# Two mixed attentions on one core: scores as a half-array and a quarter-array product, two heads at a time, and part of the local attention moved into the projections

## The chip, the core and the metric

The kernel runs on one core of a Trainium2 chip. The core has TensorE (matmuls, `PE` in the profile, its weight loads `PEld`), VectorE (`DVE`), ScalarE (`ACT`), GpSimd (`POOL`), and SyncE (`SP`), whose queue issues nearly all DMAs here. The metric is the device time of one execution in microseconds, the median of several runs.

## The reference

`x` has 2048 rows of 448. Two multi-head attentions of 16 heads of 28 are computed from it, with weights of their own, and mixed by a gate:

```python
g = sigmoid((x * gate_w).sum(-1, keepdims=True))
a = A(x, A_wqkv, A_wo)      # local: each position sees 8 positions, itself and every second one before it
b = B(x, B_wqkv, B_wo)      # full: softmax(q k^T / sqrt(28)) v over all 2048 positions
out = g * a + (1 - g) * b
```

## The kernel before

**Precision.** A matmul operand is split into a high part in a rounded 32-bit type (`F32R`) and a low part, the rest. A product is the sum of three: high x high, high x low, low x high. The product of attention weights and values alone is a plain float32 matmul, which the profile counts as two instructions.

**Projections.** 92 tiles in the order of a list `tiles`: 28 of q and k of B, transposed (`qk_tile`), 16 of v of B (`v_tile`), 48 of q, k, v of A (`a_tile`). Each is 11 matmuls (`project`, `L241`) into one of four PSUM banks `R`, copied out by ScalarE. q and k of B go to DRAM in two parts (`qk_hi`, `qk_lo`), those of A to `a_scr`. From tile 11 on each tile is followed by `s1_quad`: four matmuls of 28 rows in the four row groups of the array (`s1_mm`, `L121`), one per head, into a four-bank tile, and one VectorE maximum over the four banks (`s1_max`, `L125`). These are approximate scores, from the high parts alone, for the row maxima that the softmax subtracts. The gate's sum is a VectorE multiply-and-sum per tile of 128 rows (`gate_tile`, `L288`), from `x` loaded once more by rows.

**Main stage.** A loop over 16 units `u` (a group of four heads, a block of 512 queries) and 16 key tiles `kt` of 128 keys: 256 steps. In a step, `scores` computes S = K Q for four heads, each 128 keys x 512 queries in one PSUM bank. A head's q and k lie in one group of 32 partitions: 28 rows of values and, in the first product, two more, where k holds ones and q the negated row maximum in its two parts. So a head is three matmuls of a quarter of the array (30, 28, 28 rows), and matmuls of different row groups run at once. Three maxima matmuls of a later unit run between them, each with its VectorE maximum, until they are done: 64 a unit are 1024, 80 x 4 = 320 come in the projections, and the other 704 take 235 steps. The order is written out by hand, first digit the head, second the product, `s` a maximum:

```python
WITH = "10 20 s0 11 21 00 30 12 22 31 01 s1 32 02 s2".split()
ALONE = "00 10 20 30 01 11 21 31 02 12 22 32".split()
```

ScalarE takes the exponential of each bank into SBUF (`L885`). `do_av` then multiplies the previous step's four tiles with V (`L851`): four heads in four column groups, 128 rows each. Seven banks rotate through `order`: a step's scores and maxima take them in the order in which the step before had used them.

**Local attention.** It runs beside the main stage, in 8 chunks of two heads: GpSimd multiplies q with each of 8 shifted k (`a_score`, `L491`) and for some adds the two halves of the products (`L496`); VectorE sums the rest in two or four reduces (`a_reduce`, `L501`); then a softmax over the 8 (`a_softmax`); then GpSimd multiplies with v and sums up (`a_av`, `L541`, `L546`). Each such operation is an item in a list per engine, with a sort key, a cost, and the items that it needs with a least distance in steps. `issue` takes, at each step, the items whose needs are met, as long as the engine's planned lateness (`late`), which falls by a planned step (2.3) each step, stays under a limit: 4.2 us for GpSimd, 0.7 for VectorE.

**End.** From two steps after the last maximum, `op_some` puts seven items of the output products into each step (`op_mm`, `L693`), and the rest follows behind the loop. Loads of the finished attention rows (`op_load_b`) are tied to fixed steps, `READY` holds items back to a step.

Of the kernel before, what the change touches and what calls it, by code (L numbers as in the profile page):

```python
# [11 lines left out]
ALU = mybir.AluOpType  # L12
# [13 lines left out]
def gated_mix_kernel(ctx: ExitStack, tc: tile.TileContext, xT, xn, gw, wA, wB, woAB, out):  # L26
# [19 lines left out]
    pp = ctx.enter_context(tc.tile_pool(name="pp", bufs=16))  # L46
# [7 lines left out]
    T = []  # L54

# [16 lines left out]
    KH = [cp.tile([128, S], F32R, name=f"KH{i}") for i in range(2)]  # L72
    KL = [cp.tile([128, S], F32R, name="KL0")]
# [6 lines left out]

    def ptile(name):
        return pp.tile([128, 512], F32, tag="P", name=name)
# [5 lines left out]
    def load_k(g, t, src):  # L88
        for h in range(4):
            r = D + 112 * g + DH * h  # L90
            dma_r(t[32 * h:32 * h + DH, :], src[r:r + DH, :])

    def load_part(u, name, src):
        g, b = divmod(u, NB)
        t = sp.tile([128, 512], F32R, name=name)
        for h in range(4):
            r = 112 * g + DH * h
            dma_r(t[32 * h:32 * h + DH, :], src[r:r + DH, 512 * b:512 * b + 512])
        return t

    Qs = {}

    def load_q(u):
        Qs[u] = load_part(u, "QH", qk_hi), load_part(u, "QL", qk_lo)
        for i in range(2):
            dma_r(Qs[u][0][DH + i::32, :], nm[u][16 * i:16 * i + 16, :].rearrange("(h q) c -> h (q c)", h=4))
# [4 lines left out]
    s1c = [0]  # L111
    s1e = 64 * NU
    finished = []

    def s1_mm(n, bank):
        u, i = divmod(n, 64)
        qs, kc, h = i // 16, i // 4 % 4, i % 4
        if i == 0 and u + 1 < NU:
            qhis[u + 1] = load_part(u + 1, "qhi", qk_hi)
        r = slice(32 * h, 32 * h + DH)  # L120
        nc.tensor.matmul(bank, qhis[u][r, 128 * qs:128 * qs + 128],  # L121
                         KH[u // NB % 3][r, 512 * kc:512 * kc + 512], start=True, stop=True)

    def s1_max(n, k, bank):
        nc.vector.tensor_reduce(MX[:, n % NMX:n % NMX + k], bank, axis=X, op=ALU.max)  # L125
        if n // 64 != (n + k) // 64:
            finished.append(n // 64)
        s1c[0] = n + k

    def s1_quad():  # L130
        n = s1c[0]
        for i in range(4):
            s1_mm(n + i, T[0][:, i, :])
        s1_max(n, 4, T[0])
# [20 lines left out]
    def max_store(u, r):  # L155
        for a in range(4):
            nc.sync.dma_start(nm[u].bitcast(F32)[:, 32 * a:32 * a + 32], r[32 * a:32 * a + 32, :])

# [7 lines left out]
    with tc.tile_pool(name="xp", bufs=1) as xp, tc.tile_pool(name="wp", bufs=2) as wp:  # L166
# [35 lines left out]
        def load_w(wi, tails=(False, True)):  # L202
            src, cols = WSRC[wi]
            if wi not in wraw:
                wraw[wi] = raw3(), ptile("wt"), sum(c1 - c0 for c0, c1 in cols)
            r, t, _ = wraw[wi]
            for tail in tails:
                o = 0
# [7 lines left out]

        def split_w(wi, kts):
            if wi not in wsets:
                wsets[wi] = [wp.tile([128, 4, 448], F32R, tag=g, name=f"{g}{wi}") for g in ("wh", "wl")]
            wh, wl = wsets[wi]  # L220
            r, t, n = wraw[wi]
            for kt in kts:
                split(wh[:, kt, :n], wl[:, kt, :n], r[:, kt, :n] if kt < 3 else t[:, :n], nc.gpsimd)
# [38 lines left out]
        def v_tile(j, ws):  # L262
            bank = next_bank()
            project(bank[:, :D], j // 4, slice(128 * (j % 4), 128 * (j % 4) + 128), ws, slice(0, D), False)
            nc.scalar.activation(V[:, j, :, 0:DH], bank[:, :D].rearrange("p (h d) -> p h d", d=DH), AF.Copy)
# [3 lines left out]
        def a_tile(i, j, ws):  # L269
            bank = next_bank()  # L270
            project(bank[:, :D], j // 4, slice(128 * (j % 4), 128 * (j % 4) + 128), ws, slice(0, D), False)
# [3 lines left out]
            nc.scalar.activation(stage[0][:, :, j % 2, :], bank[:, :D].rearrange("p (c e) -> p c e", e=56), AF.Copy)  # L275
            if j % 2 == 1:
                nc.sync.dma_start(a_own[i][:, :, j - 1:j + 1, :].rearrange("c p j e -> p c j e"), stage[0])

        gwt = cp.tile([128, D], F32, name="gwt")
        gx = {}  # L280

        def gate_load(j):
            gx[j] = ptile("xg")
            nc.sync.dma_start(gx[j][:, :D], xn[:, j, :])

        def gate_tile(j):
            jk = ptile("xj")
            nc.vector.scalar_tensor_tensor(jk[:, :D], gx.pop(j)[:, :D], 1.0, gwt, op0=ALU.mult, op1=ALU.mult,  # L288
                                           accum_out=zt[:, j:j + 1])
# [4 lines left out]
        WSRC = [None, (wB, [(128, 448), (832, 896)]), (wB, [(704, 832)]),  # L294
                (wB, [(896, 1344)]), (wA, [(0, 448)]), (wA, [(448, 896)]), (wA, [(896, 1344)])]

        wh0 = wp.tile([128, 4, 448], F32R, tag="wh", name="wh0")
        wl0 = wp.tile([128, 4, 448], F32R, tag="wl", name="wl0")
# [45 lines left out]
        for i, k, nb in ([(0, k, nb) for nb, k in ((0, 1), (0, 0), (0, 2), (1, 1), (1, 2), (1, 0), (2, 1), (3, 1),  # L344
                                                   (2, 0), (2, 2), (3, 0), (3, 2))]
                         + [(i, k, nb) for i in (1, 2) for nb in range(NB) for k in range(len(QK[i]))]):
            tiles.append((i, "qk", nb, QK[i][k], 128 * k))
        for j in range(NJ):
            tiles.append((3, "v", j))
        for i in range(3):  # L350
            for j in range(NJ):
                tiles.append((4 + i, "a", i, j))
# [6 lines left out]
        loads = {2: 17, 3: 22, **{wi: firsts[wi - 1] for wi in (4, 5, 6)}}  # L359
        splits = {1: firsts[1] - 4, 2: firsts[2] - 4, 3: firsts[3] - 4, **{wi: firsts[wi - 1] + 2 for wi in (4, 5, 6)}}  # L360
        for n, t in enumerate(tiles):
# [4 lines left out]
            for w in splits:  # L366
                if splits[w] <= n < splits[w] + 2:
                    split_w(w, (2 * (n - splits[w]), 2 * (n - splits[w]) + 1))
            if n == 1:
# [8 lines left out]
            else:  # L378
                a_tile(t[2], t[3], ws)
            if n in (2, 3):  # L380
                load_w(1, (n == 3,))
            if n == 4:
                init_kh(KH[0])
            if n == 7:
                load_k(0, KH[0], qk_hi)
                qhis[0] = load_part(0, "qhi", qk_hi)
            if n == 8:
                nc.sync.dma_start(gwt, gw)
# [3 lines left out]
            if n == 9:  # L392
                init_kh(KH[1])
                nc.gpsimd.memset(V[:, :, :, DH:], 1.0)
            if n == 22:
                load_k(1, KH[1], qk_hi)
            if n == 62:
                load_k(0, KL[0], qk_lo)
# [3 lines left out]
            if finished and n < len(tiles) - 2:  # L402
                u = finished.pop(0)
                parts.append((u, max_parts(u)))
            if S1_START <= n < len(tiles) - 1:
                s1_quad()
            if 26 <= n < 58 and n % 2 == 0:
                gate_load((n - 26) // 2)
            if 29 <= n < 61 and n % 2 == 1:
                gate_tile((n - 29) // 2)  # L410
            if n == 64:
# [5 lines left out]
            if n == 65:  # L417
# [13 lines left out]

    hooks = {}

    def at(pos, st, f):
        hooks.setdefault((st, pos), []).append(f)

    def run(pos, st):
        for f in hooks.pop((st, pos), ()):
            f()


# [6 lines left out]

# [571 lines left out]
```

## Time and profile before

| | |
|---|---|
| median of 3 runs | 962.66 us (961.21 to 963.15) |
| profiled execution | 962.09 us, its span 960.3 us |
| granted TensorE clock | 0.996 |
| busy: PE, PEld | 947.0 us (99%), 553.0 us (58%) |
| busy: DVE, ACT, POOL | 746.2 (78%), 647.7 (67%), 521.9 (54%) |
| first and last score matmul (`L882`) | 280.8 us, 926.2 us after the start |

Busy time is the union of an engine's instructions. Matmuls overlap, so TensorE's 99% does not say that it is at its peak: what one slot of the array takes is read from the starts in the timeline. The busy share is a mean over stages with different limits, so the prediction reads each stage alone.

### The profile page before, as it was taken

Reading aid. Unit: us, or ns where it says so; the run is one execution under the profiler, and the core shown is the slowest. Engines: PE = TensorE matmul, PEld = TensorE weight load, DVE = VectorE, ACT = ScalarE, POOL = GpSimd, SP = SyncE. Lnnn points to the kernel's source line nnn. Section 1 sums busy time; section 2 is a strip of 40 time slices with the busy share of each in tenths; the row PEclk is TensorE's granted clock in tenths of the full one; section 3 lists DMA queues with packets and bytes.
Section 4 is the critical chain, followed back from the end, with each engine's and each line's share of the span. In section 5 each row is a group of like instructions: output and inputs, shape, how many; then the busy total and the mean of one; then the engine's idle time right before and its main releaser. Section 6 shows DMA issues by size and latency. Waiting matters only on the chain.

```text
span 960.3 us, 19993 instructions
## 1 busy us (share of the span) xinstructions
PE 947.0 (99%) x7578; PEld 553.0 (58%) x7578; DVE 746.2 (78%) x1166; ACT 647.7 (67%) x1309; POOL 521.9 (54%) x384
## 2 busy tenths in 40 slices
PE   8999999999999999999999999999999999999988
PEld 6766777777764544445444444444444444465657
DVE  6477888887779999999999999999998888400012
ACT  4434212122139999999999999999999999856541
POOL 1346101010018689999999999999993853100000
PEclk9999999999999999999999999999999999999999
DMA  9868414354246241314515331520312123344332
GB/s 277 284 199 251 137 48 126 108 135 127 77 117 212 67 126 50 89 47 118 157 42 124 108 88 37 167 72 22 107 43 51 33 68 111 111 141 127 110 102 90
DMA packets 102392, 108.15 MB, mean 113 GB/s; under 512 B 60844, under 2 KB 72636, under 8 KB 101400
## 3 DMA queue, kind: packets, MB, share of 16 engines
q1 hardware_dynamic: 102152, 106.62, 38.4%
q8 instruction: 59, 0.97, 0.4%
q10 hardware_dynamic: 144, 0.26, 0.1%
q14 instruction: 37, 0.30, 0.1%
HBM read 65.89 MB, written 40.48 MB: 111 GB/s over the span
## 4 chain that ended last, share of the span: by engine, by line
PE 87%; DMA 5%; DVE 3%; POOL 2%; SPq 1%; ACT 1%; issue 1%; ACTq 0%; DVEq 0%
PE av L851 25%; PE r L241 19%; PE r L882 15%; PE T L882 11%; PE T L121 6%; PE r L693 4%; PE T L693 4%; PE r L121 3%; DVE MX L125 2%; DMA kt<-a_scr 1%; DMA oal<-oa_scr 1%; PE r L671 1%; SPq L85 1%; POOL prod L541 1%; POOL oat L546 1%
## 5 line engine op out<-in xcount | busy, mean ns | idle before, releaser
L125 DVE TENSOR_REDUCE MX<-T 128x1 f32<-128x512 f32 (+1 forms) x384 | 384.6, 1021 | 59.6 <-PE T L121 54.5
L885 ACT ACTIVATE P<-r 128x512 f32<-128x512 f32 x581 | 329.8, 609 | 53.6 <-PE r L882 32.5
L125 DVE TENSOR_REDUCE MX<-r 128x1 f32<-128x512 f32 x400 | 262.5, 686 | 22.4 <-PE r L121 16.5
L851 PE MATMUL av<-P,V 128*32 128x512 f32 x2048 | 273.6, 606 | 0.4 <-ACT osb L708 0.4
L885 ACT ACTIVATE P<-T 128x512 f32<-128x512 f32 x443 | 255.7, 610 | 19.8 <-PE r L882 11.1
L121 PE MATMUL T<-KH,qhi 28*128 28x512 f32 x624 | 169.9, 475 | 0.9 <-DVE MX L125 0.6
L882 PE MATMUL r<-QH,KH 30*128 30x512 f32 x581 | 166.5, 471 | 1.2 <-ACT ast L275 0.6
L121 PE MATMUL r<-KH,qhi 28*128 28x512 f32 x400 | 162.6, 455 | 0.0
L882 PEld LDWEIGHTS r<-QH,KH 30*128 30x128 f32 x581 | 75.4, 183 | 125.5 <-DVE MX L125 111.3
L882 PE MATMUL T<-QH,KH 30*128 30x512 f32 x443 | 146.2, 472 | 1.0 <-ACT P L885 0.5
L882 PE MATMUL r<-QL,KH 28*128 28x512 f32 x581 | 141.8, 394 | 0.0
L882 PE MATMUL r<-QH,KL 28*128 28x512 f32 x581 | 141.4, 392 | 0.0
L491 POOL TENSOR_TENSOR prod<-qt,kt 128x896 f32<-128x896 f32 x64 | 135.0, 2114 | 7.1 <-DMA kt<-a_scr 7.0
L882 PE MATMUL T<-QL,KH 28*128 28x512 f32 x443 | 120.6, 395 | 0.0
L882 PE MATMUL T<-QH,KL 28*128 28x512 f32 x443 | 119.9, 392 | 0.0
L546 POOL TENSOR_TENSOR oat<-oat,prod 128x896 f32<-128x896 f32 x56 | 118.1, 2110 | 2.4
L882 PEld LDWEIGHTS T<-QH,KH 30*128 30x128 f32 x443 | 59.8, 182 | 91.5 <-DVE MX L125 86.5
L275 ACT ACTIVATE ast<-r 128x448 f32<-128x448 f32 x48 | 26.1, 545 | 106.7 <-PE r L241 102.3
L541 POOL TENSOR_TENSOR prod<-vt,L 128x896 f32<-128x896 f32 x56 | 95.5, 1705 | 0.7
L121 PEld LDWEIGHTS T<-KH,qhi 28*128 28x128 f32 x624 | 70.9, 182 | 35.9 <-DVE MX L125 27.6
L851 PEld LDWEIGHTS av<-P,V 128*32 128x32 f32 x2048 | 40.3, 108 | 67.6 <-issue 62.1
L681 DVE TENSOR_TENSOR oalo<-r,oah 128x384 fp32r<-128x384 f32 x16 | 8.9, 558 | 90.3 <-ACT onhi L680 80.6
(127 smaller groups left out, 1438.8 us busy)
## 6 DMA issues: line engine op xcount, KB each, us to landing
a_scr<-ast SPq DMA_DIRECT2D x24, 448.0 KB
qk_hi<-qkh SPq DMA_DIRECT2D x24, 256.0 KB
qk_lo<-qkl SPq DMA_DIRECT2D x24, 256.0 KB
rbc<-rs SPq DMA_DIRECT2D x60, 64.0 KB
KH<-qk_hi SPq DMA_DIRECT2D x16, 224.0 KB
qhi<-qk_hi SPq DMA_DIRECT2D x64, 56.0 KB
xg<-in_xn SPq DMA_DIRECT2D x16, 224.0 KB
KL<-qk_lo SPq DMA_DIRECT2D x16, 224.0 KB
```

Of the source, the lines that this page charges most:

```text
L85: nc.sync.dma_start(dst.bitcast(F32), src.bitcast(F32))
L121: nc.tensor.matmul(bank, qhis[u][r, 128 * qs:128 * qs + 128], KH[u // NB % 3][r, 512 * kc:512 * kc + 512], start=True, stop=True)
L125: nc.vector.tensor_reduce(MX[:, n % NMX:n % NMX + k], bank, axis=X, op=ALU.max)
L241: nc.tensor.matmul(bank, wa if wfirst else xa, xa if wfirst else wa, start=(i == 0), stop=(i == len(ORDER) - 1))
L275: nc.scalar.activation(stage[0][:, :, j % 2, :], bank[:, :D].rearrange("p (c e) -> p c e", e=56), AF.Copy)
L491: nc.gpsimd.tensor_tensor(out=p, in0=qt[c], in1=kvt["k", c % 2][:, HALO - DIL * w:HALO - DIL * w + NJ, :], op=ALU.mult)
L541: nc.gpsimd.tensor_tensor(out=dst.rearrange("p j (h d) -> p j h d", d=DH), in0=kvt["v", c % 2][:, HALO - DIL * w:HALO - DIL * w + NJ, :].r ...
L546: nc.gpsimd.tensor_tensor(out=oat[c], in0=oat[c], in1=oat[c, w], op=ALU.add)
L693: nc.tensor.matmul(bank[:, :D], src, wo[c][:, k, :], start=(first and k == ks[0] and i == 0), stop=(last and k == ks[-1] and i == 2))
L851: nc.tensor.matmul(av[32 * h:32 * h + 32, :], V[:, kt, 4 * g + h, :], tiles_[h], start=(kt == 0), stop=(kt == NJ - 1), skip_group_check=True)
L882: nc.tensor.matmul(held[a], (KH[g % 3], KH[g % 3], KL[g % 2])[t][r, ks], (qh, ql, qh)[t][r, :], start=(t == 0), stop=(t == 2))
L885: nc.scalar.activation(p, held[a], AF.Exp, scale=SCALE)
```

## The change

Three things are changed together.

1. **Scores.** The three products of a head become two. `wide`: a head's high and low k lie in two groups of 32 partitions next to each other, in one half of the array, with the high q beside both; one matmul of 60 rows (62 for two of the heads) sums high x high, low x high and the two rows of the maximum. `narrow`: high k x low q, 28 rows, in a quarter. Heads 0 and 1 have their tiles in one pair (`KT[..][0]`), heads 2 and 3 in another. A step does two heads first, then the other two, the pairs taking turns; the maxima matmuls use the row groups that `narrow` leaves free. K tiles now have two places, with one more (`KS`) for the maxima of group 2, and q has two places of three tiles (`QT`).
2. **Local scores of chunks 0 and 1 in the projections.** The projections' order changes: q and k of A for channels 0 to 3 (16 tiles) come after the first 12 tiles, V comes last. The local items with negative keys are issued from tile 28 on; their tiles lie in the place of V until V is written. GpSimd now adds halves once for even shifts (two reduces left) and twice for odd ones and for chunks 0 and 1 (one reduce left).
3. **Gate.** `gate_w` is two more columns of a projection's weights (450 columns); ScalarE copies the sum out.

With these go: a planned step of 2.2 for 2.3, an exponential buffer split into 11 and 5 tiles, K loads at other steps, and the output stage's loads and `READY[1, 3]` two to four steps later.

```diff
-    WITH = "10 20 s0 11 21 00 30 12 22 31 01 s1 32 02 s2".split()
-    ALONE = "00 10 20 30 01 11 21 31 02 12 22 32".split()
...
+        first = (0, 1) if st % 2 == 0 else (2, 3)
+        then = (2, 3) if st % 2 == 0 else (0, 1)
...
+        def wide(h):
+            held[h] = free.pop(0)
+            r = slice(0, 60) if h < 2 else slice(0, 62)
+            r = slice(r.start + 64 * (h % 2), r.stop + 64 * (h % 2))
+            nc.tensor.matmul(held[h], KT[g % 2][h // 2][r, ks], qa[h // 2][r, :], start=True, stop=False)
+
+        def narrow(h):
+            r = slice(HB[h], HB[h] + DH)
+            nc.tensor.matmul(held[h], KT[g % 2][h // 2][r, ks], ql[r, :], start=False, stop=True)
+            p = ptile("P")
+            nc.scalar.activation(p, held[h], AF.Exp, scale=SCALE)
+            cur[h] = p
...
+        for h in first:
+            wide(h)
+        for h in first:
+            narrow(h)
+        yield
+        if more_s1:
+            maxima(then[0], "s0")
+            maxima(then[1], "s1")
+        for h in then:
+            wide(h)
+        for h in then:
+            narrow(h)
+        if more_s1:
+            maxima(first[st // 2 % 2], "s2")
+            order[:] = [held[x] for x in (first[0], "s0", first[1], "s1", then[0], "s2", then[1])]
...
+    KT = [[cp.tile([128, S], F32R, name=f"K{i}{p}") for p in range(2)] for i in range(2)]
+    HB, LB = (0, 64, 32, 96), (32, 96, 0, 64)
...
+    def load_q(u):
+        t = QT[u % 2]
+        for p in range(2):
+            for base in (HB, LB):
+                load_part(u, t[p], qk_hi, base, (2 * p, 2 * p + 1))
+            for i in range(2):
+                dma_r(t[p][HB[2 * p] + DH + i::64, :],
+                      nm[u][16 * i + 8 * p:16 * i + 8 * p + 8, :].rearrange("(h q) c -> h (q c)", h=2))
+        load_part(u, t[2], qk_lo, HB)
...
+    at("pre", 12, lambda: load_k(2, qk_hi, HB, KS[0]))
+    for st, g, src, base in ((30, 1, qk_lo, LB), (72, 2, qk_hi, HB), (84, 2, qk_lo, LB),
+                             (129, 3, qk_hi, HB), (136, 3, qk_lo, LB)):
...
+        n = DH
+        for _ in range(3 - NR(c, w)):
+            n //= 2
+            nc.gpsimd.tensor_tensor(out=p[:, :, 0:n], in0=p[:, :, 0:n], in1=p[:, :, n:2 * n], op=ALU.add)
...
+    def NR(c, w):
+        return 1 if c < EC or w % 2 else 2
...
+        add_a(1)
+        tiles.extend((i, "qk", nb, rows, 128 * k) for i in (2, 3) for nb in range(NB) for k, rows in enumerate(QK[i]))
+        add_a(4)
+        add_a(5)
+        tiles.extend((6, "v", j) for j in range(NJ))
...
+            if n > D:
+                nc.scalar.activation(zt[:, j:j + 1], bank[:, D:D + 1], AF.Copy)
...
+            if n >= firsts[2]:
+                st = n - len(tiles)
+                if t[1] == "qk":
+                    late["pool"] += 1.3
+                issue("sp", st, 0)
+                if not any(0 <= n - splits[w] + 2 < 4 for w in splits):
+                    issue("pool", st, 5.2)
+                issue("dve", st, DLIM)
...
-    READY[1, 3] = OP0 + 22
+    READY[1, 3] = OP0 + 26
...
-            step = 2.3 if left else 2.1
+            step = 2.2 if left else 2.1
```

562 lines of the change are left out of this document (288 added, 274 removed).

## The prediction

> **What bounds the kernel now.** I read the page first, then the busy time by stage, then single steps in the timeline, then the groups by shape.
>
> ```profile
> PE 87%; DMA 5%; DVE 3%; POOL 2%; SPq 1%; ACT 1%; issue 1%; ACTq 0%; DVEq 0%
> ```
>
> This is the chain that ended last: 87% of it is TensorE. The later projections, and the main stage up to the end of the row maxima (behind it lie 109 us of steps with output products, and 28 us of end that the change doesn't touch):
>
> ```profile
> 139.00:281.00 142.00, 140.64 (x730) 105.28 (x731) 117.72 (x77) 31.54 (x66) 10.44 (x12) 1.00 0.42 114
> 281.00:823.00 542.00, 540.83 (x5351) 261.45 (x5349) 506.50 (x951) 497.65 (x994) 464.39 (x324) 1.00 0.32 90
> ```
>
> Columns are PE, PEld, DVE, ACT, POOL, granted clock, DMA share, GB/s. The second row is 56% of the span, with all four engines over 85% busy. The `av` products tell its steps (eight instructions each):
>
> ```profile
> 281.00:823.00 542.00, 247.76 (x1856) 36.56 (x1856) 1.00 0.32 90
> ```
>
> 1856/8 = 232 steps; 542/232 is 2.34, and without the 2 to 4 us of start-up about 2.32 us a step. One step on TensorE:
>
> ```profile
> 604.39 1.06 PE L851 MATMUL av<-P,V 128*32 128x512 f32 x8
> 605.38 0.50 PE L882 MATMUL r<-QH,KH 30*128 30x512 f32 x2
> ...
> 605.71 0.50 PE L882 MATMUL T<-QH,KH 30*128 30x512 f32 x1
> 605.72 0.40 PE L882 MATMUL r<-QL,KH 28*128 28x512 f32 x2
> ...
> 605.96 0.39 PE L882 MATMUL r<-QH,KL 28*128 28x512 f32 x1
> ...
> 606.20 0.38 PE L121 MATMUL T<-KH,qhi 28*128 28x512 f32 x1
> ...
> 606.30 0.49 PE L121 MATMUL T<-KH,qhi 28*128 28x512 f32 x1
> 606.72 0.64 PE L851 MATMUL av<-P,V 128*32 128x512 f32 x4
> ```
>
> Matmuls of different row groups start together; a group's next one starts 0.34 us after the first (0.50 long, weights loaded in the open) and 0.24 after any other. So 2.33 = 0.99 (`av`, and the change to scores) + 0.34 + 0.24 + 0.24 + 0.10 (the group that came late: its first matmul starts at 605.71, not 605.38) + 0.42 (drain and change to `av`). Four slots for 15 quarter-array matmuls, one group entering a slot late: TensorE's own structure, and not far above the other engines. After the maxima the twelve score matmuls fill three slots:
>
> ```profile
> 888.77 0.39 PE L882 MATMUL r<-QL,KH 28*128 28x512 f32 x1
> ...
> 889.00 0.39 PE L882 MATMUL r<-QH,KL 28*128 28x512 f32 x1
> ...
> 889.34 1.06 PE L851 MATMUL av<-P,V 128*32 128x512 f32 x8
> ```
>
> There the slots are 0.23, and the last leaves for `av` after 0.34, not 0.42. The prices of the other engines, first the exponentials and the gate:
>
> ```profile
> L885 ACT ACTIVATE P<-r 128x512 f32<-128x512 f32 x581 | 329.8, 609 | 53.6 <-PE r L882 32.5 <-PE T L882 17.7
> ...
> L288 DVE SCALAR_TENSOR_TENSOR xj<-xg,gwt 128x448 f32<-128x448 f32 x16 | 10.8, 678 | 0.0
> ```
>
> The local scores and products, by tile (ns: least, median, most; first and last start in us):
>
> ```profile
> L501 DVE TENSOR_REDUCE L<-prod x176: 327/376/380, 303.0 to 715.1; 128x8 f32<-128x224 f32 x96, 128x16 f32<-128x224 f32 x80
> L491 POOL TENSOR_TENSOR prod<-qt,kt x64: 2099/2112/2150, 291.4 to 707.0; 128x896 f32<-128x896 f32 x64
> L541 POOL TENSOR_TENSOR prod<-vt,L x56: 1692/1703/1731, 359.3 to 774.8; 128x896 f32<-128x896 f32 x56
> L546 POOL TENSOR_TENSOR oat<-oat,prod x56: 2093/2110/2138, 362.3 to 776.6; 128x896 f32<-128x896 f32 x56
> L496 POOL TENSOR_TENSOR prod<-prod x40: 1018/1024/1037, 293.6 to 709.2; 128x448 f32<-128x448 f32 x40
> ```
>
> **The change, part by part.** The sum stands against the profiled execution: 962.1 us, its span 960.3 and 1.8 around it, 0.06% under the median of three.
>
> *Scores.* Per step 12 quarter-array matmuls become 4 `wide` ones (60 or 62 rows, two at a time fill the array) and 4 `narrow` ones (28 rows). The order is two wide; two narrow with two maxima in the other two row groups; two wide; two narrow with the third maximum. That is four slots again, but no group enters late. If half and quarter tiles follow each other as quarters do now: 0.99 + 0.34 + 0.24 + 0.24 + 0.34 = 2.15; with 0.42 at the end 2.23. The last matmul is a maximum, as in the step above, so I take the upper part, 2.21. (2.32 - 2.21) x 235 = **-26 us**; bounds -45 (2.13, slots of 0.23 as from 888.77 to 889.00) and 0 (2.32).
>
> For this no other engine may stand above 2.21. ACT: two exponentials take 1.09 (below), each is 0.61 long, so the second starts 0.48 after the first; 4 x 0.48 = 1.92, and the 994 - 4 x 232 = 66 other activations, at about 0.5, add 0.14: 2.06. DVE: 506.5 - 104 local reduces (176 before in this stage, 72 after) x 0.37 - 10 short softmax instructions of two chunks, the same 0.37 taken = 464, /235 = 1.98. POOL: 464, less 16 products x 2.11 = 34 and about 4 of softmax, plus 8 (48 halvings of 448 elements for 40, at 1.02) and 12 (24 of 224 elements, about 0.5 each, an estimate on the line through 1.02 for 448 and 2.11 for 896): 446. Its local work ended at 778.7 (last `L546` start and length, above), 498 us for 464, so 446 takes some 478 and ends near 760, ahead of the output products. All fit, POOL closest: while local work lasts, about 210 steps, it needs some 2.1 a step.
>
> ```profile
> 603.73 1.32 DVE L125 TENSOR_REDUCE MX<-r 128x1 f32<-128x512 f32 x2 [0.30 <-PE r L121]
> ...
> 605.16 1.09 ACT L885 ACTIVATE P<-T 128x512 f32<-128x512 f32 x2
> ```
>
> *Waits it adds.* A bank passes from a maximum to a wide score of the next step: the second of the later two heads takes the third maximum's bank, used 0.58 after the step's start. VectorE gets the first two maxima about 0.34 + 0.39 after the step's start, and three follow at some 0.63 (two in 1.32 above, about 0.69 each), so that bank is free about 2.7 after it: 2.21 + 0.58 = 2.79 is just later. A step with two local reduces (0.37 each) misses it by some 0.3, with the later scores and `av` queued behind; at a tenth of the steps that is 0.03 a step, inside the 0.06 that I took above 2.15.
>
> *Last 21 steps (no maxima).* Three slots become four: +0.24 x 21 = **+5**. Bounds 0 to +10. Output work waits for step 250, not 246. The four more steps without it have 2.15 of TensorE work beside 2.06 of ACT, so next to nothing idles, and what is put off runs behind the loop at the same price: **0**, bounds -3 to +4.
>
> *Projections.* The number of tiles stays; half of the local q and k comes third, V last. The first `av` needs V a step after the last tile, and ACT copies it within a tile: 0. Sixteen small V fills on POOL and 16 column copies on ACT (31.5 of 142 busy) lie beside TensorE: 0. The gate leaves VectorE (16 x 0.68, and its loads, 16 of 224 KB) and becomes 2 of 450 columns: 16 x 11 x 0.001 = 0.2 us of TensorE. VectorE gets 16 reduces and 10 of softmax: 10 us for 11. POOL gets 16 x (2.11 + 1.02 + 0.5) = 58, and two more K fills, in a stage where it is busy 10.4 of 142. The cover is TensorE's 2.9 us a tile. Behind a product on POOL stand weight splits (wanted 16 tiles later) and the low parts of q and k; 11 P buffers at 3 a tile give 3.7 tiles, over 10 us, against a delay of one product and its halvings, 3.6. If the cover is gone, a tile waits on VectorE: 26 x 0.37 = +10 at worst. I take **0**, bounds -2 to +10.
>
> *Queues.* SP issues 16 loads a q tile instead of 10, and local k, q loads among projection stores; it isn't on the chain (1%). K tiles have two places and one for maxima; the tightest, group 3, is asked for at step 129 and first wanted at (768 - 320)/3 = 149, 44 us later. **0**, up to +4 for a late load.
>
> Sum: 962.1 - 26 + 5 = **941**.
>
> **The rivals.**
>
> *A, half and quarter tiles drain the array between them (slower).* What a change of shape costs, rows of a projection around four quarter matmuls:
>
> ```profile
> 183.12 0.78 PE L241 MATMUL r<-wh,xl 128*128 128x448 f32 x3
> 183.87 0.51 PE L121 MATMUL T<-KH,qhi 28*128 28x512 f32 x4
> 184.31 0.68 PE L241 MATMUL r<-wh,xh 128*128 128x448 f32 x2
> ```
>
> The third matmul starts at 183.12 + 0.78 - 0.37 = 183.53, the next full one at 184.31: 0.78 for two slots of 0.21, and the second full one 0.31 later instead of 0.20. So 0.47 for two changes, 0.23 each. A step has two now (`av` to scores and back) and would have five: 2.21 + 0.69 = 2.90, 235 x 0.58 = +136, and 21 x 0.93 = +20: about 1118. It decides from 0.04 us a change (3 x 0.04 = the 0.11 gained). Against it, a change of column count alone goes without a break:
>
> ```profile
> 844.50 0.66 PE L671 MATMUL r<-ident,oal 128*128 128x128 f32 x4
> 844.91 0.65 PE L693 MATMUL r<-wo,oah 128*128 128x448 f32 x2
> ```
>
> The fourth of these transposes has 64 columns, and four of 0.11 fill 844.50 to 844.91. No row of this trace has a 64-row tile beside a 32-row one.
>
> The Trainium skill, TensorEngine Tiling (Array Packing), Tiling Modes, says that changing the tiling mode, not just the tile, drains TensorE, and lists 64 and 32 rows as different modes: by that rule, A. The trace agrees for full array against quarters (0.23) and shows nothing for halves.
>
> *B, no drain, but weights can't be loaded ahead across the two sizes.* A slot with open weights is 0.34 for 0.24: three more, +0.30: 2.51, 235 x 0.19 = +45, tail 21 x 0.54 = +11: 1018. Against it, quarters load ahead during a matmul of their own group now:
>
> ```profile
> 605.38 0.18 PEld L882 LDWEIGHTS r<-QH,KH 30*128 30x128 f32 x2 [0.84 <-DVE MX L125]
> ...
> 605.49 0.19 PEld L882 LDWEIGHTS r<-QL,KH 28*128 28x128 f32 x2
> ```
>
> *C, the step isn't TensorE's.* The idle of 0.84 in that row is put down to VectorE; if the maxima set the step, packing gains only what VectorE and POOL lose. At 2.32 unchanged: 962.1 + 5 = 967. Against: from `av` to scores it is 0.99 here, with the weights loaded as the scores start, which a wait that varies would not give; VectorE loses 42 us anyway. Half of the gain, 2.27, gives 955.
>
> **How the numbers follow.** Likeliest, 915 to 957: 0.70 (low end: 2.13 a step, -45, and -2 from the other terms' lower bounds). C 0.09, a third each in 957 to 960, within 2 us of before, and near 967. A 0.13, B 0.08. This kernel's runs tell about 0.2%, 2 us, from no change: faster 0.73, same 0.03, slower 0.24. The range 914 to 972 takes in the likeliest and C, 0.79, and a little of a mild B; A and B are left out.
>
> **What would show it.** Right: in the middle stage `av` starts follow at 2.15 to 2.25; narrow matmuls start 0.34 after the wide ones and the next wide ones 0.24 later; VectorE near 464 and POOL near 446 us busy there; the projection tiles keep 2.9; the steps without maxima longer by 0.24. Wrong: 0.4 or more between wide and narrow with 0.49-long narrow matmuls (A; with 0.34 each, B); TensorE idle before the second wide pair on VectorE (the bank) or VectorE idle on POOL; projection tiles over 3 us with waits on POOL.

## The result and the profile after

| | median us | runs | ratio to before |
|---|---|---|---|
| before | 961.93 | 4 (960.28 to 963.15) | |
| after | 1118.54 | 4 (1096.90 to 1197.87) | 1.1408 [1.1375, 1.1441] |

The changed kernel is slower, where 941 us was forecast. Its executions differ because the granted clock does, and the ratio compares the two with the highest clock (1096.90 and 1097.52 us); the execution profiled here took 1139.56, but from 400 to 920 us its clock is full, and there it can be read beside the kernel before. Its page, first the granted clock in 40 slices, then the chain that ended last, then the two costliest groups of score matmuls:

```profile
PEclk8999999999555799999999999999999999895799
...
PE 96%; DMA 2%; DVE 1%; SPq 1%; issue 0%; ACT 0%
...
L955 PE MATMUL r<-Q,K 60*128 60x512 f32 (+1 forms) x512 | 136.6, 528 | 0.6 <-ACT V L491 0.6
L959 PE MATMUL T<-Q,K 28*128 28x512 f32 x512 | 136.5, 529 | 0.0
```

TensorE holds 96% of the chain, for 87% before, and the clock has two holes, one at the start of the main stage and one near the end. By stage (PE, PEld, DVE, ACT, POOL, granted clock, DMA share, GB/s):

```profile
139.00:270.00 131.00, 129.94 (x673) 97.71 (x670) 111.56 (x80) 31.90 (x82) 75.18 (x82) 1.00 0.38 105
...
300.00:320.00 20.00, 20.00 (x82) 5.83 (x82) 8.70 (x15) 8.89 (x17) 19.45 (x14) 0.50 0.28 70
...
400.00:920.00 520.00, 520.00 (x3625) 173.32 (x3627) 390.37 (x692) 410.71 (x813) 384.42 (x277) 1.00 0.28 75
...
960.00:1137.00 177.00, 163.31 (x783) 95.69 (x781) 21.63 (x50) 68.44 (x145) 4.28 (x5) 0.86 0.28 86
```

The same 20 us of the kernel before:

```profile
300.00:320.00 20.00, 20.00 (x207) 9.82 (x199) 19.27 (x38) 17.78 (x35) 19.53 (x14) 1.00 0.28 71
```

The projections (first row) go on as before, with the local products now in POOL's column. In the main stage the other engines fall to 74 to 79% busy: TensorE alone holds the step. One step, from the timeline of all engines:

```profile
600.57 1.07 PE L933 MATMUL av<-P,V 128*32 128x512 f32 x8
...
601.57 0.50 PE L955 MATMUL r<-Q,K 60*128 60x512 f32 x2
602.00 0.18 PEld L959 LDWEIGHTS r<-Q,K 28*128 28x128 f32 x2 [0.24 <-issue]
602.00 0.50 PE L959 MATMUL r<-Q,K 28*128 28x512 f32 x2
...
602.44 0.49 PE L955 MATMUL T<-Q,K 62*128 62x512 f32 x2
...
602.86 0.50 PE L959 MATMUL T<-Q,K 28*128 28x512 f32 x2
...
603.29 1.06 PE L933 MATMUL av<-P,V 128*32 128x512 f32 x8
```

From `av` to `av` are 2.72 us. The slots start at 601.57, 602.00, 602.44 and 602.86, 0.43 apart where quarters among themselves take 0.23 or 0.24; the matmuls are all 0.50 long, and the weights of the next size load only as its matmuls start. That is the sign given for A. The step's median (steps 10 to 220, as below) is 2.725, and at full clock it hardly varies: 1.00 + 4 x 0.43 = 2.72.

Where the profiled execution's 177 us went, by the start of the first `av`, of the one 224 steps later, and the end of the span:

| us | first `av` | 224 steps on | end |
|---|---|---|---|
| before | 284.8 | 805.6 | 960.3 |
| after | 287.7 | 938.7 | 1137.7 |
| quarters_end (below) | 283.5 | 804.7 | 957.5 |
| fill_first_unit (below) | 288.5 | 905.8 | 1074.6 |

That is 2.9 before the loop, 130.2 in the 224 steps (224 x 0.40 = 90, and 40 at half clock) and 44.3 behind them.

### The profile page after: what moved, and what is told of

The parts are those of the page before. It is cut to its first block, busy times and chain, and to the rows that moved or that the text cites. A ratio compares the mean times of both kernels' runs of the same rounds, so it can differ in the third digit from the quotient of the medians.

```text
span 1137.7 us, 18097 instructions
## 1 busy us (share of the span) xinstructions
PE 1116.3 (98%) x6554; PEld 522.4 (46%) x6554; DVE 715.7 (63%) x1046; ACT 657.5 (58%) x1325; POOL 576.5 (51%) x468
## 4 chain that ended last, share of the span: by engine, by line
PE 96%; DMA 2%; DVE 1%; SPq 1%; issue 0%; ACT 0%
PE av L933 24%; PE r L466 20%; PE r L955 10%; PE T L955 10%; PE T L959 10%; PE r L959 10%; PE T L142 3%; PE r L775 3%; PE T L775 3%; PE r L753 1%; DVE MX L147 1%; DMA V<-in_xT 1%; DMA oal<-oa_scr 0%; DMA onhi<-on_hi 0%; SPq L96 0%; DMA onlo<-on_lo 0%
## 5 line engine op out<-in xcount | busy, mean ns | idle before, releaser
L961 ACT ACTIVATE P<-r 128x512 f32<-128x512 f32 x512 | 278.0, 595 | 204.9 <-PE r L142 133.0
L955 PEld LDWEIGHTS r<-Q,K 60*128 60x128 f32 (+1 forms) x512 | 50.6, 194 | 228.2 <-ACT P L961 218.8
L955 PE MATMUL r<-Q,K 60*128 60x512 f32 (+1 forms) x512 | 136.6, 528 | 0.6 <-ACT V L491 0.6
L959 PE MATMUL T<-Q,K 28*128 28x512 f32 x512 | 136.5, 529 | 0.0
L955 PE MATMUL T<-Q,K 62*128 62x512 f32 (+1 forms) x512 | 136.2, 528 | 0.0
L959 PE MATMUL r<-Q,K 28*128 28x512 f32 x512 | 136.0, 527 | 0.0
L142 PE MATMUL T<-K,qhi 28*128 28x512 f32 x470 | 121.1, 507 | 1.1 <-DVE MX L147 1.0
L955 PEld LDWEIGHTS T<-Q,K 62*128 62x128 f32 (+1 forms) x512 | 50.6, 194 | 68.2 <-issue 57.5
L142 PE MATMUL r<-K,qhi 28*128 28x512 f32 x298 | 81.1, 535 | 0.0
L466 PE MATMUL r<-wh,xh 128*128 128x448 f32 (+1 forms) x256 | 69.3, 392 | 0.0
```

What stands on the lines that cost most here:

```text
L142: nc.tensor.matmul(bank, qhis[u][r, 128 * (i // 4):128 * (i // 4) + 128], s1_keys(u // NB, h)[r, 512 * (i % 4):512 * (i % 4) + 512], start ...
L466: nc.tensor.matmul(bank, wa if wfirst else xa, xa if wfirst else wa, start=(i == 0), stop=(i == len(ORDER) - 1))
L955: nc.tensor.matmul(held[h], KT[g % 2][h // 2][r, ks], qa[h // 2][r, :], start=True, stop=False)
L959: nc.tensor.matmul(held[h], KT[g % 2][h // 2][r, ks], ql[r, :], start=False, stop=True)
L961: nc.scalar.activation(p, held[h], AF.Exp, scale=SCALE)
```

## The experiments

### The sizes: is it the change between them?

**quarters.** The changed kernel with a head's scores as three quarters again, in K and q tiles as before, two heads first, in four full slots:

```diff
-        for h in first:
-            wide(h)
-        for h in first:
-            narrow(h)
...
+            a, b = first
+            c, d = then
+            part(a, 0), part(b, 0), maxima(c, "s0"), maxima(d, "s1")
+            part(a, 1), part(b, 1), part(c, 0), part(d, 0)
+            part(a, 2), part(b, 2)
+            yield
+            part(c, 1), part(d, 1), part(c, 2), part(d, 2)
```

> The changed kernel with its gate, local part, projections and queues as they are, but each head's three products in its own quarter again (K and q tiles laid out as before): two heads start with two maxima beside them, the other two heads a slot later, 15 quarter matmuls in four slots. Theory 'size change' (the array empties and the weights load in the open whenever 64-row and 32-row tiles follow each other, 0.2 us each): only two changes a step are left, TensorE needs 0.99 + 0.34 + 0.23 + 0.23 + 0.34 = 2.13, and with waits for banks 2.2 to 2.3 a step: 935 to 955 us, the clock back within 10 us of the start of the main stage. Rival 'the rest' (the time was lost in the local part, the gate or the queues): the step stays over 2.6 and the time over 1060.

Measured: 973.36 us (ratio 1.0125 [1.01, 1.015]), step 2.33. The local part and the gate are those of the changed kernel, and the 2.725 is gone: the sizes made it. But the time lies above the 935 to 955 expected. Four full slots with no late group do not give 2.15 either, so the gain was missed for a second reason, and some 13 us are lost outside the loop. Both are followed below.

**four_wide.** All four `wide`, then `narrow` and maxima: a size changes once inside a step.

```diff
-        for h in first:
+        for h in (*first, *then):
             wide(h)
...
-        for h in then:
-            wide(h)
```

> The changed kernel with the four wide matmuls first and then the four narrow ones with the maxima: the same matmuls, one change from 64 to 32 rows a step instead of three changes. Theory 'size change': 1.00 + 0.34 + 0.33 + 0.34 + 0.33 = 2.34 a step, 2.35 to 2.45 with waits for banks, 990 to 1015 us in all. Rival 'same bank' (a narrow matmul waits because the wide one just before it wrote the same bank): every narrow one now has another pair between, so all slots but the first are 0.23: 2.13, 2.2 to 2.3 with waits, 950 to 975 us. Rival 'half tile' (a 64-row tile takes 0.43 whatever follows): 0.43 from the first wide pair to the second, 2.5 or more a step, over 1030 us.

Measured: 1013.62 us (1.0543 [1.0515, 1.0571]), step 2.43, for 2.725 with three changes. Its scores (timeline of TensorE):

```profile
602.23 0.50 PE L955 MATMUL r<-Q,K 60*128 60x512 f32 x1
...
602.57 0.40 PE L955 MATMUL r<-Q,K 62*128 62x512 f32 x1
...
602.95 0.50 PE L959 MATMUL r<-Q,K 28*128 28x512 f32 x1
...
603.29 0.39 PE L959 MATMUL r<-Q,K 28*128 28x512 f32 x1
```

A second wide pair behind the first is 0.40 long and 0.34 later, the first narrow one again 0.50 long and 0.38 later (0.33 in the median of the steps): weights load ahead within a size and not over a change. One change on a step without any, 2.13, would make 2.33. The 0.10 above that goes with a wait for VectorE: in 209 of the 210 steps one of the maxima's matmuls starts 0.05 to 0.06 after a VectorE maximum ends, in the median 0.11 behind the others of its slot.

**halves.** `narrow` on the rows of a whole half too, the maxima in a slot of their own behind them: five slots, one change. It adds low k times another head's low q.

```diff
-            r = slice(HB[h], HB[h] + DH)
+            r = slice(0, 60) if h < 2 else slice(0, 62)
+            r = slice(r.start + 64 * (h % 2), r.stop + 64 * (h % 2))
...
```

> The changed kernel with the narrow matmuls widened to the 60 or 62 rows of the wide ones (the added rows of q are zeros or another head's low parts, so the sum changes by about a millionth), and the three maxima in a slot of their own behind them. Same banks, same order of heads, but wide and narrow have one size. Theory 'size change': wide to narrow to wide in 0.23 a slot; 1.00 + 0.34 + 3 x 0.23 + 0.33 (to the quarters) + 0.42 = 2.8 with the slot of the maxima, or about 2.75, so no faster than the changed kernel, but 0.23 between wide and narrow. Rivals 'same bank' and 'half tile': 0.43 between wide and narrow as in the changed kernel, 3.1 a step or more.

Measured: 1034.65 us (one run), step 2.56, below the 2.75 expected, whose sum has a slot of 0.23 too many. Its timeline of TensorE:

```profile
601.51 0.50 PE L955 MATMUL r<-Q,K 60*128 60x512 f32 x1
...
601.85 0.39 PE L960 MATMUL r<-Q,K 60*128 60x512 f32 x1
...
602.08 0.40 PE L955 MATMUL r<-Q,K 62*128 62x512 f32 x1
...
602.32 0.39 PE L960 MATMUL r<-Q,K 62*128 62x512 f32 x1
...
602.65 0.50 PE L142 MATMUL r<-KS,qhi 28*128 28x512 f32 x1
...
603.09 1.06 PE L933 MATMUL av<-P,V 128*32 128x512 f32 x8
```

Half tiles follow each other like quarters, 0.34 and then 0.23 and 0.24, also where `narrow` writes the bank that the `wide` just before it wrote; so neither a half tile as such nor the shared bank makes the 0.43. The quarter maxima come 0.33 after the last half tile, and stand 0.44 for themselves: the change costs 0.10 in the slot before it, and 0.10 in the open weights of the slot behind it.

**wide_twice.** Each pair of `wide` issued twice, the second adding the same again: as many changes, two more slots within a size.

```diff
-        for h in first:
+        for h in (*first, *first):
...
-        for h in then:
+        for h in (*then, *then):
```

> The changed kernel with each wide matmul issued twice (its scores count the wide product twice). The number of size changes stays, the streaming in a step grows by two slots of 0.23: about 3.2 us a step at full clock, 1200 us in all. It is for the clock, which in the profile of the changed kernel is half for 96 us from the start of the main stage, where before it was half for 3.4 us. Theory 'too little streaming': the clock stays down while the share of time in which the array streams is too small; with two slots more it comes back within 10 us. Rival 'size changes themselves, or the power of the chip': it stays down as long as in the changed kernel or longer.

Measured: 1199.93 us (one run), step 3.19: 0.23 for each added slot, at full clock through the main stage (window of 320 to 1000 us):

```profile
320.00:1000.00 680.00, 680.00 (x4903) 241.11 (x4899) 435.60 (x772) 479.36 (x912) 420.16 (x303) 1.00 0.23 61
```

So the 0.43 is not the price of a `wide`, it is a `wide` with a change behind it, 0.43 - 0.23 = 0.20. Three changes on a step without them (2.13, half_both below) are 2.13 + 0.60 = 2.73.

### The 13 us outside the loop

**quarters_end.** quarters with the output work at the steps that the kernel before had:

```diff
-    READY[1, 3] = OP0 + 26
+    READY[1, 3] = OP0 + 22
...
-        at("end", OP0 + 9 + k, lambda k=k: op_load_b(0, k))
+        at("end", OP0 + 7 + k, lambda k=k: op_load_b(0, k))
```

> The kernel of quarters (973 us) with the end of the kernel before: loads of the output stage and the item held back at the same steps as before (250 becomes 246 again). In quarters the last attention product starts at 920.5 us, as before (921.6), but the span is 12 us longer: the output products that were put off run behind the loop. Theory 'held back' (the four steps without output work are what costs the 12 us): 960 to 963 us, no difference from before that could be measured. Rival 'the end is longer for another reason' (last loads, the moved P buffers): 968 to 975 us.

Measured: 959.63 us (12 runs), 0.9986 [0.9974, 0.9999]: within 0.2% of before, and 13.7 us under quarters. Only the output work, its loads and the item held back were moved. The windows of quarters, then of quarters_end:

```profile
840.00:920.00 80.00, 72.25 (x491) 41.67 (x495) 4.74 (x13) 41.30 (x85) 2.79 (x3) 0.94 0.32 97
920.00:972.00 52.00, 46.84 (x267) 38.59 (x259) 11.87 (x26) 14.08 (x33) 0.00 (x0) 0.99 0.37 118
```

```profile
840.00:920.00 80.00, 78.92 (x561) 49.05 (x560) 6.97 (x19) 45.41 (x96) 2.82 (x3) 1.00 0.45 134
920.00:957.00 37.00, 32.81 (x185) 27.10 (x183) 9.63 (x20) 9.22 (x22) 0.00 (x0) 1.00 0.23 75
```

Held back, the products leave TensorE idle for 8 of these 80 us, with 70 fewer matmuls done, and what is put off makes the stretch behind 15 us longer. Some of it can be the clock's: in the profile of quarters it is half for 10 us here (0.94), which can cost up to 5 us.

### What held the step of quarters at 2.33

The stage of quarters_end is ahead of before in all that parts 2 and 3 of the change were to do:

```profile
281.00:821.00 540.00, 539.55 (x5335) 278.03 (x5336) 470.91 (x836) 496.62 (x991) 448.64 (x324) 1.00 0.31 83
```

VectorE has 36 us less than before (506.50), POOL 16 less (464.39), and the step did not move.

**before_early.** The kernel before, with the late head's first product (`30`) fourth in the order, not seventh, and the second and third maxima last:

```diff
-    WITH = "10 20 s0 11 21 00 30 12 22 31 01 s1 32 02 s2".split()
+    WITH = "10 20 s0 30 11 21 00 31 12 22 01 32 02 s1 s2".split()
```

> The kernel before, with only the written order of a step changed: 10 20 s0 30 / 11 21 00 31 / 12 22 01 32 / 02 s1 s2, so that the fourth row group starts with the others and every slot is full. Theory 'late group' (the prediction's reading: the step of 2.32 has 0.10 from the group that enters late): 2.2 a step, 935 to 945 us. Rival 'banks' (a step waits until ScalarE has freed a PSUM bank, and comes to about 2.3 however the slots are packed; quarters had full slots and 2.32): 2.27 to 2.33 a step, 952 to 965 us.

Measured: 976.54 us (1.0166 [1.0143, 1.019]), step 2.385; neither theory had it slower. From the timeline of all engines:

```profile
600.51 0.68 DVE L125 TENSOR_REDUCE MX<-T 128x1 f32<-128x512 f32 x1
...
600.76 0.50 PE L882 MATMUL r<-QH,KH 30*128 30x512 f32 x2
...
600.77 0.49 PE L882 MATMUL T<-QH,KH 30*128 30x512 f32 x1
...
601.10 0.39 PE L882 MATMUL r<-QL,KH 28*128 28x512 f32 x2
...
601.25 0.18 PEld L882 LDWEIGHTS T<-QH,KH 30*128 30x128 f32 x1 [0.19 <-DVE MX L125]
601.25 0.50 PE L882 MATMUL T<-QH,KH 30*128 30x512 f32 x1
```

`30` now starts with the others (600.77), so the first slot is full. What comes late is `00`, 0.49 after the first score. By the order of the banks it takes the one that the third maximum of the step before used, and VectorE ends that maximum at 600.51 + 0.68 = 601.19; `00` starts 0.06 later. In 207 of the 210 steps a first product starts 0.05 to 0.06 after a maximum ends. The edit filled the slot, but it also moved the maxima to the end of the step, and with them the wait for VectorE.

The late group of the kernel before is this wait too. Beside the step that the prediction shows stands

```profile
604.97 0.68 DVE L125 TENSOR_REDUCE MX<-T 128x1 f32<-128x512 f32 x1
```

which ends at 605.65, and `30`, which there takes that bank, starts at 605.71. A first product starts 0.05 to 0.06 after a maximum in 205 of the 210 steps. So the group is late because VectorE is, and not because it is written seventh.

**half_exp, half_max, half_both.** The kernel before with shorter work on the banks: exponentials over half the columns (`av` reads these twice), maxima over half the columns, and both.

```diff
...
-                nc.scalar.activation(p, held[a], AF.Exp, scale=SCALE)
+                nc.scalar.activation(p[:, 0:256], held[a][:, 0:256], AF.Exp, scale=SCALE)
```

```diff
-        nc.vector.tensor_reduce(MX[:, n % NMX:n % NMX + k], bank, axis=X, op=ALU.max)
+        nc.vector.tensor_reduce(MX[:, n % NMX:n % NMX + k], bank if k == 4 else bank[:, 0:256], axis=X, op=ALU.max)
```

> The kernel before, with the exponential of only the first 256 of the 512 columns, which the attention product then reads twice (so half of the attention weights are left out); matmuls, maxima and order as before. ScalarE frees a bank sooner and is far from its limit. Theory 'banks': the step falls to 2.13 to 2.2, the time to 920 to 940 us. Rival 'late group' (TensorE's own order sets the step): the step stays at 2.3 and the time at 955 to 962 us.

> The kernel before, with the main stage's 704 row maxima over the first 256 of 512 columns (the other half is left out), all else as before. half_exp brought the step only from 2.32 to 2.30, before_early made it 2.39. Theory 'VectorE's bank' (a score waits for the bank that a maximum holds, and the reduces of the local part push the maxima back): VectorE has 0.3 us less a maximum, the step falls to 2.15 to 2.22, 935 to 945 us. Rival 'TensorE's order' (the late group, 2.25 to 2.3): the step stays at 2.3.

> The kernel before with half of the exponentials' and half of the maxima's columns (both as above): no bank is held long. What is left is TensorE's own order. Theory 'late group': 2.25 to 2.3 a step. Rival (the late group costs nothing, waits for banks alone do): 2.13 to 2.18.

Measured (one run each): 954.3, 962.03 and 944.37 us; steps 2.295, 2.336 and 2.13. Alone they do next to nothing, together they take off 0.19, with the matmuls and their written order untouched (half_both's time holds short spells at half clock, mean step 2.28; its median step is taken at full clock). Its timeline of TensorE:

```profile
760.76 1.07 PE L851 MATMUL av<-P,V 128*32 128x512 f32 x8
761.76 0.50 PE L883 MATMUL r<-QH,KH 30*128 30x512 f32 x2
...
762.89 0.64 PE L851 MATMUL av<-P,V 128*32 128x512 f32 x4
```

The traces show two waits, one for each engine. Beside the wait of `30` for VectorE, the last maximum's matmul (`s2`) takes the bank of the last exponential, and starts 0.05 to 0.06 after an exponential ends in 163 of the 210 steps before. Shorter exponentials remove the second wait (5 steps) and leave the first (203); shorter maxima remove the first (0; `30` now starts 0.02 after the first score, in the median, and the step is 2.336 all the same) and leave the second (114). Only half_both has neither (3 and 5).

**quarters_half_both, quarters_half_exp, quarters_half_max.** The same three on quarters_end, where VectorE has 36 us less to do.

> The kernel of quarters_end (959.6 us, 2.32 a step) with half of the exponentials' and half of the maxima's columns. Its slots are full and no group enters late. If its 2.32 is waits for banks: 2.13 to 2.16 a step, 915 to 925 us. If TensorE takes 2.3 for 15 quarter matmuls and the attention product however they stand: 2.3.

> quarters_end with the exponentials over 256 of 512 columns (the product with V reads these twice); maxima whole. VectorE is busy 437.86 of 500 us there, 36 us less than in half_exp, where it was 473 of 500. Theory 'ScalarE sets the step' (two exponentials in 1.09 us, four are 2.06 us a step with the rest): step 2.13 to 2.17, and about 920 us. Theory 'VectorE or its banks': 2.30 to 2.33, about 955. Theory 'a ring of banks that ScalarE and VectorE hold in turn': between, 2.20 to 2.28, about 930 to 945; half_exp's 2.295 is then VectorE at 95%.

> quarters_end with the maxima over 256 of 512 columns, exponentials whole. 'ScalarE sets the step': 2.31 to 2.33 and 957 to 960 us, as half_max against before. 'VectorE or its banks': 2.13 to 2.17, about 920. 'A ring of banks': 2.20 to 2.28, about 930 to 945.

Measured (one run each): 918.79, 937.56 and 958.51 us; mean steps 2.17, 2.235 and 2.318 (medians 2.133, 2.255 and 2.332). Shorter maxima change nothing in either kernel: ScalarE's part alone holds the 2.33. Shorter exponentials give 0.09 by the means (2.324 to 2.235; 0.07 by the medians), and shorter maxima 0.07 (0.12) more on top: VectorE comes right behind. The windows of half_exp and of quarters_half_exp, 300 to 800 us (third column VectorE, fourth ScalarE):

```profile
300.00:800.00 500.00, 495.28 (x4995) 209.88 (x4996) 473.23 (x901) 283.19 (x925) 444.52 (x301) 1.00 0.31 83
```

```profile
300.00:800.00 500.00, 500.00 (x5150) 210.33 (x5148) 452.35 (x807) 294.27 (x956) 438.49 (x316) 1.00 0.30 80
```

In half_exp VectorE is at 95%, and the exponentials alone bring 0.03 there by the medians, and 0.07 where parts 2 and 3 of the change have relieved VectorE: 954.3 against 937.56 us. What the change takes from VectorE, together with the other order of the slots, is worth some 17 us (one run each), but only behind a shorter ScalarE. The theory "ScalarE sets the step" has quarters_half_max right and quarters_half_exp wrong by 0.07 (2.13 to 2.17 expected); the ring of banks has it the other way round.

ScalarE's rows in quarters_half_max, and two of TensorE's, show how it holds a step that it is not busy for:

```profile
601.28 1.08 ACT L949 ACTIVATE P<-r 128x512 f32<-128x512 f32 x2 [0.18 <-PE r L946]
...
602.25 1.10 ACT L949 ACTIVATE P<-T 128x512 f32<-128x512 f32 x2
...
603.40 0.50 PE L135 MATMUL T<-KH,qhi 28*128 28x512 f32 x1
...
603.64 1.08 ACT L949 ACTIVATE P<-r 128x512 f32<-128x512 f32 x2 [0.29 <-PE r L946]
...
603.83 1.07 PE L923 MATMUL av<-P,V 128*32 128x512 f32 x8
```

Its last exponential ends at 603.35, when the next step's scores (from 602.58) are not finished: it waits 0.29 for TensorE, and has the four exponentials of a step ahead of it again. 2.06 of work and a wait of 0.2 to 0.3 are the 2.33. TensorE in turn waits for the bank of that last exponential. By the order of the banks the third maximum's matmul takes it, and that matmul starts at 603.40, 0.05 after the exponential ends; `av` starts 0.43 behind it. In 205 of the 210 steps it starts 0.05 to 0.06 after an exponential ends, in quarters_end in 207, and in quarters_half_exp and quarters_half_both, where the step is shorter, in none. From there the loop runs through two steps: 0.05 + 0.43 + 1.00 (`av` to scores) + 1.06 (scores to the first exponential) + 2.07 (four exponentials) = 4.61, or 2.31 a step. In some steps the last head's first score waits for the exponential before it as well, and no run separates these two waits.

A row that misleads here, from the waits of quarters_half_both, 300 to 800 us (total, times, longest):

```profile
PEld r L947 <- ACT P L950: 194.2, 227, 3.4
```

At 2.133 a step, with ScalarE 60% busy, TensorE's wait for it stands there as large as in quarters (184.5 from 290 to 800): the wait is the 0.84 in which `av` runs, and it names whoever came last before that.

### The changed kernel itself: the clock

**after_end.** The changed kernel with the output work at the steps of before (the lines shown at quarters_end).

> The changed kernel with the end of the kernel before (the held-back item at step 246, the loads two to four steps sooner). Theory 'held back': 8 to 14 us less than the changed kernel's 1097. Theory 'too little streaming' for the clock: the runs still differ from one another by tens of us, with a granted clock below 0.98, since the order of the steps is the changed kernel's. Rival: the end doesn't matter here, the same 1097.

Measured: 1126.22, 1088.99, 1068.17 and 1168.52 us, at mean clocks of 0.937, 0.975, 0.998 and 0.898. The time near full clock, 1068.17, is 107 over before, and the other executions take up to 100 us more, the more the lower their clock. At nearly the same clock, 1088.99 (0.975) stands against 1096.90 (0.976) in the changed kernel: 8 us, the low end of what was expected of the output work. A stretch at half clock, from the profile of after (timeline of TensorE):

```profile
311.56 1.93 PE L933 MATMUL av<-P,V 128*32 128x512 f32 x8
313.42 0.79 PE L955 MATMUL r<-Q,K 62*128 62x512 f32 x2
314.15 0.79 PE L959 MATMUL r<-Q,K 28*128 28x512 f32 x2
```

That is 4.77 a step, for 96 us from 286 us on.

**fill_first_unit.** after_end with `wide` issued twice in the first 16 steps (their scores count it double):

```diff
-        for h in first:
+        twice = 2 if st < 16 else 1
+        for h in first * twice:
...
```

> The kernel of after_end with each wide matmul issued twice in the first 16 of the 256 steps (those scores count the wide product twice). after_end ran 1068 us at a granted clock of 0.998 and 1089 to 1169 at 0.975 to 0.898. Theory 'too little streaming': the clock falls at the start of the main stage and comes back only when the array streams enough; with the first steps filled it comes back at once and stays, as it stays in the changed kernel once it is back: every run at 1074 to 1080 us (1068 and 16 x 0.47), clock over 0.99. Rival (the clock falls at random, whatever the first steps do): runs spread over 1070 to 1170 again.

Measured: 1075.8 us (4 runs, 1075.13 to 1076.46; 1.1164 [1.1114, 1.1214]), clock 0.997. Its windows:

```profile
300.00:320.00 20.00, 20.00 (x149) 7.11 (x145) 12.72 (x22) 13.43 (x26) 19.45 (x14) 1.00 0.27 71
...
289.00:936.00 647.00, 647.00 (x4518) 216.75 (x4510) 475.73 (x840) 508.02 (x1004) 449.46 (x323) 1.00 0.28 76
```

7 us of added work in 16 steps keep the clock at 1.00 there and in the 600 us behind them, and take the spread over four runs from 100 us to 1.3. It also gives the accounting at full clock, from the table above: 3.7 before the loop, 224 x 0.40 = 90 and 7 of filling, 14 behind: 114.3 in the profiled spans.

No version here beats the kernel before by more than 0.2% without leaving work out.

## Why the prediction was wrong

- **Scores, the step that failed.** "If half and quarter tiles follow each other as quarters do now: 0.99 + 0.34 + 0.24 + 0.24 + 0.34": they don't. A slot between two changes is 0.43, and the step 2.725 for 2.21. Quarters follow each other so, and halves do among themselves (halves), but not the one behind the other.
- **What bounds the kernel, the reading that failed with it.** Of the 2.33 I put 0.10 for the late group and 0.42 at the end down to "TensorE's own structure". half_both keeps the matmuls and their written order and takes 2.13. In the step that the prediction shows, the 0.10 is a wait for ScalarE: the last slot's matmul starts at 606.30, 0.05 after the exponential ends (605.16 + 1.09 = 606.25), where 606.20 was due. Its weights are then in the open (0.49 long), which is 0.10 of the 0.42; in half_both the last slot takes 0.32. The late group itself waits for VectorE. So even without a price of change the -26 would not have come: quarters_end, with full slots, is at 2.33. The argument against C, that 0.99 from `av` to scores doesn't vary, was right in its number and looked at the wrong place: the waits lie at the late group and before `av`, not there. I had ScalarE at 2.06 and called it a fit; it is 2.06 and a wait.
- **Rival A had the mechanism.** Its price of 0.23 a change, read from full array against quarters, was 0.20 for halves against quarters, and stands on 2.13, not 2.21: 2.73, where A said 2.90. Its 1118 beside the measured median of 1118.54 is chance: near full clock the kernel stands at 1068 (after_end), with the held-back output work at 1076 to 1082 (an estimate, from the 8 and the 13.7 us above), and the rest goes with the clock (0.88 to 0.977), which no part of the prediction had.
- **B** came in as half of it: the weights in the open are 0.10 of the 0.20 (halves).
- **Held-back output work:** "runs behind the loop at the same price: 0, bounds -3 to +4" was 13.7, of which up to 5 may be the clock's. TensorE idles in the steps without that work, 8 of 80 us.
- **Last steps:** +5 was 14 behind the 224 steps in fill_first_unit, 3 of it in steps that still have maxima.
- **What held.** Projections 0: the first `av` at 283.5 in quarters_end, for 284.8. VectorE in that run's main stage 471 for a forecast of 464, POOL 449 for 446. A halving of 224 elements was estimated at 0.5 us and took 0.71:

```profile
L235 POOL TENSOR_TENSOR prod<-prod 128x224 f32<-128x224 f32 x24 | 17.0, 709 | 1.9
```

- **Open.** Whether another order of the banks, without shorter work, would bring the step under 2.33: no run has one with the waits taken out. And why the clock stays low in after and after_end (below).

## What to carry to other kernels

Count the changes of tile size in the order of matmuls, not the slots: one between half and quarter tiles cost nearly as much here as a whole slot (0.20 for 0.23), so a packing pays only where equal sizes stand together. Before a step is called an engine's own, shorten the others' work in it, both at once and each alone: in a loop of engines that wait for each other the busy shares don't name the limit (in the window of quarters_half_exp TensorE's row is full, 500.00 of 500.00 us, and the step still falls with shorter maxima), and the wait that the profile names may be there with or without the limit. Read instead which start follows which end by a constant time. And keep work that fills gaps where the gaps are: put off by two to four steps it cost up to 13.7 us, though nothing was added.

## What the runs showed of the hardware

- A change between 64-row and 32-row tiles costs 0.20 us at 512 columns, 0.10 in the slot before it and 0.10 in weights that load in the open behind it; between tiles of one size there is none (0.23 a slot for halves as for quarters). The Trainium skill, TensorEngine Tiling (Array Packing), Tiling Modes, says that a change of mode drains TensorE; the trace agrees for 64 against 32 rows, and has the price.
- In after the clock fell to half at the start of the main stage and stayed there for 96 us with TensorE's row busy throughout (20.00 of 20.00 us; the ends of matmuls are modelled). It fell for 133 us in after_end's profile, for 3.4 us at the same place in the kernel before, and not at all there in fill_first_unit, whose first 16 steps have two more matmul slots each. The Trainium skill, TensorE: Matmul & The Clock Gate, What's actually happening, has half clock after an idle window of some 3.4 us and full clock after a busy one; no such idle stretch stands in the row here, so by that rule alone the 96 us are not explained. wide_twice, with the same number of changes, kept 1.00 through its main stage, and so did halves; what decides it was not found.
- A matmul can start before others that are written ahead of it, when its own row group and bank are free: in half_max `30`, written seventh, starts at 601.30, 0.02 after the first of the step, and `11` and `21`, written fourth and fifth behind `10` and `20` in their row groups, at 601.62.
